# Rows of experts 2 to 7 by way of DRAM and turned on VectorE, and low parts of expert weights formed on VectorE

## The chip, the cores and the metric

The kernel runs on one core of one Trainium2 chip. A core has five engines that run side by side: TensorE (PE in the profile, with its weight loads as PEld), VectorE (DVE), ScalarE (ACT), GpSimd (POOL) and SyncE (SP); here SP only issues DMAs, and POOL issues the indirect ones. The metric is the device time of one execution in microseconds, lower is better. The time before is the median of three runs.

## The reference, cut to what matters

Attention over 8 batches of 2496 tokens with 256 features, then a mixture of 8 experts over all 19968 tokens. All data are float32.

```python
# attention, per batch
scores = (1.0 / S) * np.matmul(z, z.transpose(0, 2, 1))
x = u * np.matmul(np.maximum(scores, 0.0) ** 2, v)
# mixture of experts, x as 19968 x 256
do_compute = x @ w_skip > 0
xc = x[do_compute]
logits = xc @ w_gate
e_idx = np.argmax(logits, axis=1)          # one expert per token
gate_w = softmax(logits)[e_idx]
for e in range(8):
    mask = e_idx == e
    h = np.maximum(xc[mask] @ w1[e], 0.0)  # 256 -> 1024
    y[mask] = gate_w[mask, None] * (h @ w2[e])
out = x.copy()
out[do_compute] = xc + y
```

With the inputs of the run, 10022 tokens go to an expert: 1191, 1245, 1235, 1194, 1290, 1073, 1292 and 1502 to the experts 0 to 7.

## The kernel before

**Precision.** Every large product is made of three PE products of a faster float type: an operand is split into a high part (a cast, on ACT) and a low part (operand minus high part, a subtraction), and high x high, high x low and low x high are summed in PSUM. So weights, activations and rows each need a cast and a subtraction.

**The two stages.** The attention stage fills the first 1260 us. It writes the rows of x to `xr` in DRAM and for each token an entry (token number, gate weight) into the list of its expert, `lst`. The expert stage follows; the change is there.

**Units.** The expert stage works through the experts in order. An expert has three fixed units of 256 tokens each (`NFIX`, two tiles of 128 rows, called a pair here), and then a switch (`tc.Switch`, one arm for each number of 64-token pieces) whose arm holds the units for the rest. In an arm, a unit covers up to 512 tokens: with these counts the arms of experts 2 to 7 hold 8, 7, 4 + 5, 5, 4 + 5 and 8 + 4 pieces, thus 5 or 6 pairs for each expert. `unit` (L609) emits four `h_part`s for a fixed unit (two blocks of 128 of the 1024 hidden features each; PE writes `psh`, ACT the high part `hh`, DVE the low part `hl`), then `y_part`s (PE, `y`), and last `o = y * gate + x` on DVE and the indirect DMA of `o` to the output on POOL. In the first unit of an arm all four first `h_part`s come ahead of the first `y_part`. `psh` has four buffers.

**What else is emitted in a unit.** `fills` maps a slot (0 to 3 after the four `h_part`s, 4 to 6 after the pieces of y, 7 behind them but ahead of `o`) to jobs. Since the order is written by hand, the slot sets the place on every engine that the job uses. The jobs:

- `rows(e, i)`: `fetch` (L580) copies 256 token numbers to `go` on DVE, and POOL gathers the rows from `xr` into the tile `pair(e, i)`, 128 rows per indirect DMA. Four `go` buffers are there.
- `turn_pe` (L596): PE transposes the pair by four transposes of 128x128 into `pst`, ACT casts it to the high part, DVE subtracts for the low part. The result `xt` (`xtf` for an expert's first pair) has the features on the partitions, as PE needs it. Pair i + 1 is turned in slot 3 of unit i, the pairs 3 and 4 both in unit 2, and pair 0 of the next expert in slot 7 of unit 2.
- `wq`, from `load_w` (L126): eight pieces of the next expert's weights, each a DMA of 256 KB by SP into `raw` (four buffers), a cast on ACT and a subtraction (`w1l`, or the second half of `w2t`). The subtraction is on DVE for expert 1's weights, and on POOL for those of experts 2 to 7, which are formed while the expert ahead of them runs.
- `load_ids`: a list from DRAM, on SP.

In one expert, rows of its own pairs 3 to 5 are gathered in slot 1 of its units 0 to 2, and those of the next expert's pairs 0 to 2 in slot 4.

Of the kernel before, what the change touches and what calls it, by code (L numbers as in the profile page):

```python
# [8 lines left out]
F32 = mybir.dt.float32  # L9
# [35 lines left out]
def f32(ap):  # L45
    return ap.bitcast(F32)
# [3 lines left out]
def attn_moe(ctx, tc, zT, uT, v, wg, w1, w2, cst, pad, out):  # L50
# [21 lines left out]
    dram = ctx.enter_context(tc.tile_pool(name="dram", bufs=1, space=bass.MemoryType.DRAM))  # L72
# [102 lines left out]
    nc.gpsimd.memset(ones, 1.0)  # L175
    psw = ps_s.tile([P, 2, QC], F32, name="psw", tag="s")
    for _ in range(NWARM):
        nc.tensor.matmul(psw[:32, 0, :70], ones[:, :32], ones[:, :70], start=True, stop=True)
# [417 lines left out]
    def turn_pe(xg, xt, n=2, o=0, rows64=False):  # L596
# [9 lines left out]
        nc.scalar.copy(xh, ps[:, :, : n * P])  # L606
        nc.vector.tensor_sub(xl, ps[:, :, : n * P], f32(xh))
# [319 lines left out]
    def add(fills, *slots):  # L927
        for k, f in slots:
            fills.setdefault(k, []).append(f)

    def rows(e, i):
        return lambda: fetch(ids_of(e, i), pair(e, i))

    for e in range(E):
        more = e + 1 < E
        wq = load_w(e + 1, nc.gpsimd if e else nc.vector) if more else []
        narms = NARM + (2 if e == 0 else 1)
        for i in range(NFIX):
            fills = {}
            if e:  # L940

                add(fills, (1, rows(e, i + 3)), (3, lambda: turn_pe(pair(e, i + 1), turned(e, i + 1))))
                if e == 1 and i == 0:
                    add(fills, (0, rows(1, 2)))
                if more:
                    add(fills, (4, rows(e + 1, i)))
                if i == 0 and e + 2 < E:
                    add(fills, (6, lambda: load_ids(idts[e + 2], e + 2, 2 * NSTAT)))
                add(fills, *zip((1, 3, 5), wq[3 * i : 3 * i + 3]))
            elif i == 0:  # L950
                add(fills, (0, lambda: turn_pe(pair(0, 1), turned(0, 1))))
                add(fills, (1, gates), (1, logits), (1, route), (2, counts), (2, gate), (2, rows0), (2, rows1),
                    (2, store), (4, store), (5, end_routes), (6, end_lists))
                add(fills, *zip((0, 2), left))
            elif i == 1:
                add(fills, (1, end_counts), (3, lambda: turn_pe(pair(0, 2), turned(0, 2))), (4, rows(0, 3)), (6, rows(0, 4)))
                add(fills, *zip((1, 3, 5), wq[:3]))
            else:
                add(fills, (1, rows(1, 0)), (3, rows(0, 5)), (4, lambda: turn_pe(pair(0, 3), turned(0, 3))),
                    (5, rows(1, 1)), (6, lambda: load_ids(idts[2], 2, 2 * NSTAT)))  # L960
                add(fills, *zip((1, 2, 3, 5, 6), wq[3:]))
            if e and more and i == 2:
                add(fills, (7, lambda: turn_pe(pair(e + 1, 0), turned(e + 1, 0))))
            if i == NFIX - 1:

                add(fills, (5, lambda: turn_pe(pair(e, NFIX + 1), turned(e, NFIX), 2, 2 * P)))
                n = nc.values_load(fin["arm"][0:1, e : e + 1], min_val=0, max_val=narms - 1)  # L967
                add(fills, (1, lambda: tc.switch_hint({g: n for g in ENGINES}, narms, label="rest%d" % e)))  # L968
            ids = ids_of(e, i) if e else idt_e[:, 2 * i : 2 * i + 2, :]
            xg = pair(e, i)  # L970
            unit(e, 4, ids, [xg[:, 0, :], xg[:, 1, :]], turned(e, i), fills)


        for arm in tc.Switch(n, narms, hint="rest%d" % e):  # L974
            ws = widths(arm) if arm <= NARM else []
            if arm > NARM:
                for i in range(NFIX):
                    xg = fetch(ids_of(0, i), xgs["u"][i])
                    turn_pe(xg, xts[0])
                    unit(0, 4, ids_of(0, i), [xg[:, 0, :], xg[:, 1, :]], xts[0])  # L980
            end = NFIX + -(-sum(ws) // 4)
            i, there = NFIX, NFIX + 2
            if e == 0 and not ws:
                turn_pe(pair(1, 0), turned(1, 0))
            for j, hw in enumerate(ws):
                fills = {}
                after = ws[j + 1 :]
                nxt = i + -(-hw // 4)
                if e == 0 and j == 0:
                    add(fills, (1, lambda: turn_pe(pair(1, 0), turned(1, 0))))  # L990
                while there < min(i + 3, end - 1):
                    there += 1
                    add(fills, (1, rows(e, there)))
                if after:
                    xt = xts[(NFIX + j + 1) % 2]
                    add(fills, (3, lambda nxt=nxt, xt=xt: turn_pe(pair(e, nxt), xt)))
                    if after[0] > 4:
                        add(fills, (5, lambda nxt=nxt, xt=xt: turn_pe(pair(e, nxt + 1), xt, 2, 2 * P)))
                w = -(-hw // 2)
                xg = [pair(e, i + t // 2)[:, t % 2, :] for t in range(w)]  # L1000
                unit(e, hw, ids_of(e, i, w), xg, xts[(NFIX + j) % 2], fills, not more and not after, 3 if j else 4)
                i = nxt
            if arm >= NARM:
                ce = nc.values_load(fin["cnt"][0:1, e : e + 1], min_val=0, max_val=N)
                with tc.For_i((NSTAT if arm == NARM else NFIX) * UT, ce, UT) as tok:
                    it = op.tile([P, 2, 2], I32, name="it", tag="it")
                    nc.sync.dma_start(
                        it, lst[bass.ds(tok + e * CAP, UT), :].rearrange("(k p) c -> p k c", p=P)
                    )
                    xg = fetch(it, xgs["u"][0])  # L1010
# [57 lines left out]
```

## Time and profile before

| | |
|---|---|
| median of 3 runs | 1759.48 us (1757.15 to 1759.67) |
| the profiled execution | 1750.08 us, of which the span is 1748.3 us |
| granted TensorE clock | 0.998 |
| busy in 0 to 1262 us | PE 1254.30, DVE 992.69, ACT 979.67, POOL 268.64 us; DMA share 0.73 |
| busy in 1262 to 1748.3 us | PE 475.62, DVE 195.14, ACT 151.87, POOL 251.17 us; DMA share 0.29 |
| DMA | 294.71 MB |

The two stretches are the attention and the expert stage. How its rows are read: a group is line, engine, operation, out<-in and count, then busy time and mean ns of one, then the idle time of the engine just ahead of them and what ended it. A row of the timeline is start and duration in us, engine, line and operation, with the idle time ahead of it in brackets. In a list of waits stand total, number and longest, in us. "DMA issues" give count, KB each and the median us from issue to landing. A line "... x4" joins four instructions.

### The profile page before, as it was taken

The page shows a single profiled execution, that of the slowest core. Times are in us where ns is not written, and L with a number is a line of the kernel's source. Part 1 is how long each engine was busy: PE and PEld are TensorE (multiplying, and loading weights), DVE is VectorE, ACT ScalarE, POOL GpSimd, SP SyncE. Part 2 cuts the span into 40 slices and gives each one's busy share as a digit, 9 for nine tenths or more (in the row PEclk, how much of TensorE's full clock was granted, in tenths as well). Part 3 has the DMA queues.
Part 4 walks back from the last instruction along what each step waited for, and adds up shares of the span by engine and source line. Part 5 has one row for each costly group of instructions (what it writes and reads, how often), then busy time and mean ns, then how long its engine had stood idle before and what let it go on. Part 6 is the DMA issues. An engine that isn't in the chain of part 4 may idle for free. (4 is left out here: it accounts for less than half of the span.)

```text
span 1748.3 us, 39163 instructions
## 1 busy us (share of the span) xinstructions
PE 1729.9 (99%) x15476; PEld 1531.0 (88%) x15476; DVE 1187.8 (68%) x1928; ACT 1131.5 (65%) x1409; POOL 519.8 (30%) x516
## 2 busy tenths in 40 slices
PE   9999999999999999999999999999999999999998
PEld 7888788988888898888889888888999999999997
DVE  7877877887887788788778877877753334344332
ACT  8877877887687778768787876887533323333321
POOL 1103202212311221231222032122256456635731
PEclk9999999999999999999999999999999999999999
DMA  5566779577867858885785888586653333323310
GB/s 194 151 180 173 187 209 275 136 221 233 216 167 202 251 162 231 230 234 148 206 250 163 212 240 228 138 223 190 202 128 81 86 88 106 91 59 97 85 42 26
DMA packets 373514, 294.71 MB, mean 169 GB/s; under 512 B 136432, under 2 KB 311409, under 8 KB 372560
## 3 DMA queue, kind: packets, MB, share of 16 engines
q1 hardware_dynamic: 359136, 267.85, 55.4%
q0 software_dynamic: 13632, 22.99, 4.6%
q8 instruction: 137, 2.24, 0.5%
q14 instruction: 177, 1.45, 0.3%
q10 hardware_dynamic: 432, 0.18, 0.0%
HBM read 177.92 MB, written 133.79 MB: 178 GB/s over the span
## 5 line engine op out<-in xcount | busy, mean ns | idle before, releaser
L366 PE MATMUL acc<-ah,vh 64*128 64x512 f32 (+1 forms) x3120 | 641.5, 384 | 2.7 <-DVE ah L335 2.0
L366 PE MATMUL acc<-ah,vl 64*128 64x512 f32 (+1 forms) x3120 | 626.4, 382 | 0.0
L339 DVE TENSOR_TENSOR al<-r,ah 128x1024 fp32r<-128x1024 f32 (+1 forms) x400 | 479.2, 1204 | 169.6 <-ACT ah L335 163.1
L366 PE MATMUL acc<-al,vh 64*128 64x512 f32 (+1 forms) x3120 | 498.2, 384 | 1.9 <-DVE al L339 1.2
L537 POOL DMA_INDIRECT lst<-pair,dest x160 | 200.0, 1250 | 769.1 <-DVE dest L535 685.1
L335 ACT CAST ah<-r 128x1024 fp32r<-128x1024 f32 (+1 forms) x356 | 362.8, 1030 | 80.9 <-PE acc L366 43.4
L366 PEld LDWEIGHTS acc<-ah,vh 64*128 64x128 f32 x3120 | 326.8, 184 | 56.0 <-ACT ah L335 4.3
L366 PEld LDWEIGHTS acc<-ah,vl 64*128 64x128 f32 x3120 | 327.1, 184 | 44.5 <-DVE vl L122 0.3
L366 PEld LDWEIGHTS acc<-al,vh 64*128 64x128 f32 x3120 | 309.5, 184 | 56.3 <-DVE al L339 11.7
L325 ACT ACTIVATE r<-ps 128x1024 f32<-128x1024 f32 (+1 forms) x248 | 252.7, 1019 | 147.2 <-PE ps L277 129.1
L643 ACT ACTIVATE hh<-psh 128x512 fp32r<-128x512 f32 (+2 forms) x172 | 97.0, 571 | 282.6 <-PE psh L638 261.2
L326 ACT ACTIVATE r<-r 128x1024 f32<-128x1024 f32 (+1 forms) x248 | 261.4, 1054 | 7.9
L657 PE MATMUL y<-w2t,hh 128*128 128x256 f32 (+1 forms) x1328 | 235.0, 280 | 0.0
L644 DVE SCALAR_TENSOR_TENSOR hl<-psh,hh 128x512 fp32r<-128x512 f32 (+2 forms) x172 | 110.2, 655 | 146.7 <-ACT hh L643 130.2
L294 DVE STREAM_TRANSPOSE rt<-r 128x512 f32<-128x512 f32 x304 | 197.3, 687 | 9.4 <-DMA kept<-rt 8.5
L657 PEld LDWEIGHTS y<-w2t,hh 128*128 128x128 f32 (+1 forms) x1328 | 200.5, 185 | 1.3
L638 PE MATMUL psh<-xt,w1h 128*128 128x256 f32 (+3 forms) x896 | 184.6, 303 | 2.9 <-DVE hl L644 2.9
L657 PE MATMUL y<-w2t,hl 128*128 128x256 f32 (+1 forms) x664 | 184.2, 277 | 0.0
L638 PEld LDWEIGHTS psh<-xt,w1h 128*128 128x128 f32 x896 | 141.7, 189 | 8.5 <-DVE hl L644 4.4
L638 PE MATMUL psh<-xt,w1l 128*128 128x256 f32 (+3 forms) x448 | 135.0, 301 | 0.0
L689 POOL DMA_INDIRECT out<-o,idt x77 | 76.5, 994 | 164.2 <-DVE o L686 131.9
L657 PEld LDWEIGHTS y<-w2t,hl 128*128 128x128 f32 (+1 forms) x664 | 122.6, 185 | 0.0
(188 smaller groups left out, 1706.7 us busy)
## 6 DMA issues: line engine op xcount, KB each, us to landing
kept<-rt SPq DMA_DIRECT2D x304, 256.0 KB, 4.8
r<-kept SPq DMA_DIRECT2D x90, 512.0 KB, 6.5
r<-kept SPq DMA_DIRECT2D x62, 352.0 KB, 5.6
raw<-in_v SPq DMA_DIRECT2D x80, 256.0 KB, 5.5
ut<-in_uT SPq DMA_DIRECT2D x32, 512.0 KB, 5.8
xr<-xrow SPq DMA_DIRECT2D x128, 128.0 KB, 3.1
out<-xr SPq DMA_DIRECT2D x32, 512.0 KB, 6.8
raw<-in_w SPq DMA_DIRECT2D x64, 256.0 KB, 3.3
```

Source lines behind the costliest of these rows:

```text
L294: nc.vector.transpose(t[:, :, 32 * k : 32 * k + 32].rearrange("p (k a) i -> p a k i", k=4), r[:, x, :].rearrange("p (a k i) -> p a k i", a ...
L325: nc.scalar.activation(r[:, :, :n], ps[:, :, :n], AF.Relu, scale=isc)
L326: nc.scalar.activation(r[:, :, :n], r[:, :, :n], AF.Square)
L335: (nc.scalar.copy if on_act(ci, p) else nc.vector.tensor_copy)(h_, r_)
L339: nc.vector.tensor_sub(l_, r_, f32(h_))
L366: nc.tensor.matmul(acc[t][:, :n], w[h, x, dd], a[h, x, :n], start=(first and t not in halves[:m]), stop=(last and t not in halves[m + 1 :]),)
L537: put = nc.gpsimd.indirect_dma_start(out=lst, out_offset=bass.IndirectOffsetOnAxis(ap=dest[:, t : t + 1], axis=0), in_=pair[:, t, :], in_o ...
L638: nc.tensor.matmul(ps[:, j * W : (j + 1) * W], wt[:, a, o : o + P], x[:, d, :W], start=(m == 0), stop=(m == 5),)
L643: nc.scalar.activation(hh[:, : G * W], ps[:, : G * W], AF.Relu)
L644: nc.vector.scalar_tensor_tensor(hl[:, : G * W], ps[:, : G * W], 0.0, f32(hh[:, : G * W]), op0=ALU.max, op1=ALU.subtract)
L657: nc.tensor.matmul(ys[t], h[:, tt], w2t[f][:, k, :], start=(f == 0 and m == 0 and t % share == 0), stop=(f == NF - 1 and m == 2), skip_gro ...
L689: put = nc.gpsimd.indirect_dma_start(out=out, out_offset=bass.IndirectOffsetOnAxis(ap=ids[:m, t, 0:1], axis=0), in_=ot, in_offset=None, bo ...
```

## The change

From expert 2 on (`FAR = 2`) a pair of rows goes through DRAM once more. `to_far` writes the gathered pair to a buffer `far` of its expert in DRAM, and `blocks` reads it back by four DMAs into a tile of 32-row blocks, so that one 32x32 block transpose on DVE (`turn_dve`) gives the turned pair, which ACT casts and DVE subtracts as before. PE has no part in it. The features come out in another order, and the rows of `w1` of these experts are put in the same order on the host. All six pairs of an expert are gathered while the expert ahead of it runs, two pairs per unit in slots 1 and 2, in tiles that alternate between two sets. All weights' low parts are formed on DVE. The PE warm-up at the kernel's start has 48 products of 77 columns instead of 52 of 70.

```diff
-NWARM = 52
+NWARM = 48
+FAR = 2
+    far = [[dram.tile([UT, D], F32, name="far%d%d" % (k, i)) for i in range(NSTAT)] for k in range(2)]
...
+    blk, more_rows = [], []
+    def blk_of(i):
+        return blk[i % 2][:, : UT // 32] if i else xgs["u"][2].rearrange("p t (m f) -> p (t m) f", f=64)
+    def blocks(e, i):
+        src = far[e % 2][i].rearrange("(m i) (b f) -> b i m f", i=32, b=4)
+        for b in range(4):
+            nc.sync.dma_start(blk_of(i)[32 * b : 32 * b + 32], src[b])
+    def to_far(e, i):
+        return lambda: nc.sync.dma_start(far[e % 2][i].rearrange("(t p) d -> p t d", p=P), pair(e, i))
+    def turn_dve(e, i, xt, o=0):
+        raw = zp.tile([P, 2 * D], F32, name="xraw", tag="zf", bufs=3)
+        nc.vector.transpose(
+            raw.rearrange("p (d m i) -> p m d i", d=2, i=32),
+            blk_of(i).rearrange("p m (d j) -> p m d j", d=2),
+        )
+        xh, xl = (x[:, :, o : o + UT] for x in xt)
+        r = raw.rearrange("p (d q) -> p d q", d=2)
+        nc.scalar.copy(xh, r)
+        nc.vector.tensor_sub(xl, r, f32(xh))
...
+    def turn(e, i, xt, o=0):
+        return (lambda: turn_dve(e, i, xt, o)) if e >= FAR else (lambda: turn_pe(pair(e, i), xt, 2, o))
+    def to_blocks(e, i):
+        return lambda: blocks(e, i)
     for e in range(E):
         more = e + 1 < E
-        wq = load_w(e + 1, nc.gpsimd if e else nc.vector) if more else []
+        wq = load_w(e + 1, nc.vector) if more else []
         for i in range(NFIX):
             if e:
-                add(fills, (1, rows(e, i + 3)), (3, lambda: turn_pe(pair(e, i + 1), turned(e, i + 1))))
+                if e < FAR:
+                    add(fills, (1, rows(e, i + 3)))
+                else:
+                    add(fills, (0, to_blocks(e, i + 1)))
+                add(fills, (3, turn(e, i + 1, turned(e, i + 1))))
                 if more:
-                    add(fills, (4, rows(e + 1, i)))
+                    add(fills, (1, rows(e + 1, 2 * i)), (2, rows(e + 1, 2 * i + 1)))
+                    if i:
+                        add(fills, (3, to_far(e + 1, 2 * i - 2)), (4, to_far(e + 1, 2 * i - 1)))
+                if e >= FAR and i == 0:
+                    add(fills, (3, to_far(e, 4)), (4, to_far(e, 5)))
+                if e >= FAR and i == NFIX - 1:
+                    add(fills, (0, to_blocks(e, NFIX + 1)), (6, to_blocks(e, NFIX + 2)))
+                if more and i == NFIX - 1:
+                    add(fills, (4, to_blocks(e + 1, 0)), (7, turn(e + 1, 0, turned(e + 1, 0))))
...
-                add(fills, (5, lambda: turn_pe(pair(e, NFIX + 1), turned(e, NFIX), 2, 2 * P)))
+                add(fills, (5, turn(e, NFIX + 1, turned(e, NFIX), 2 * P)))
...
+    w1 = np.concatenate([moe_w1[:FAR], moe_w1[FAR:, cols]])
```

In the arms `turn` stands in the place of `turn_pe` in the same way.

DVE in unit 2 of expert 3, from the third hl to o, in the program before (`xt1` is the pairs 3 and 4 turned for the arm, `xtf` the first pair of expert 4):

```order
L644 SCALAR_TENSOR_TENSOR hl_40854<-psh_40852,hh_40853 128x512
L644 SCALAR_TENSOR_TENSOR hl_40871<-psh_40869,hh_40870 128x512
L607 TENSOR_TENSOR xt1_17733<-pst_40886,xt1_17733 128x2x256
L584 COPY go_40911<-idt4_204 128x2
L607 TENSOR_TENSOR xt1_17733<-pst_40931,xt1_17733 128x2x256
L607 TENSOR_TENSOR xtf_18114<-pst_40962,xtf_18113 128x512
L686 SCALAR_TENSOR_TENSOR o_40969<-y_40763,idt3_203,xgf_18108 128x256 x2
```

And the same place in the changed program:

```order
L673 SCALAR_TENSOR_TENSOR hl_40911<-psh_40909,hh_40910 128x512
L586 COPY go_40926<-idt4_216 128x2
L673 SCALAR_TENSOR_TENSOR hl_40936<-psh_40934,hh_40935 128x512
L629 STREAM_TRANSPOSE xraw_40951<-blk_18126 128x8x2x32
L636 TENSOR_TENSOR xt1_17745<-xraw_40951,xt1_17745 128x2x256
L161 TENSOR_TENSOR w2t_40956<-raw_40757,w2t_40956 128x256
L161 TENSOR_TENSOR w2t_40959<-raw_40757,w2t_40959 128x256
L629 STREAM_TRANSPOSE xraw_40991<-blk_18125 128x8x2x32
L636 TENSOR_TENSOR xt1_17745<-xraw_40991,xt1_17745 128x2x256
L629 STREAM_TRANSPOSE xraw_41023<-xgu_18123 128x8x2x32
L636 TENSOR_TENSOR xtf_18131<-xraw_41023,xtf_18130 128x512
L715 SCALAR_TENSOR_TENSOR o_41027<-y_40812,idt3_215,xgf_18120 128x256 x2
```

Between the last hl and o stood three subtractions and a copy; now there are three transposes, three subtractions of turned rows and two of weights.

SP in expert 3, from its last weights to the switch, in the program before (`raw` is a piece of expert 4's weights):

```order
L578 DMA idt5_205<-lst_88 128x16x2
L97 DMA raw_40621<-in_w2 128x512
L97 DMA raw_40668<-in_w2 128x512
L97 DMA raw_40708<-in_w2 128x512
L967 TENSOR_LOAD arm_18374
L967 ISA x2
L968 SWITCH_STRIDE
L968 ISA
```

And in the changed program, from the last piece of weights on (`far00` to `far03` are pairs 0 to 3 of the successor expert, `far13` to `far15` pairs 3 to 5 of the running one, `xgu_18123` and `blk` the block tiles):

```order
L99 DMA raw_40757<-in_w2 128x512
L1019 TENSOR_LOAD arm_18391
L1019 ISA x2
L621 DMA blk_18126<-far13_100 32x8x64 x4
L621 DMA blk_18125<-far14_101 32x8x64 x4
L1020 SWITCH_STRIDE
L1020 ISA
L1020 BRANCH_PREFETCH_HINT
L624 DMA far02_91<-xgf_17743 128x2x256
L624 DMA far03_92<-xgx_18127 128x2x256
L621 DMA xgu_18123<-far00_89 32x8x64 x4
L621 DMA blk_18126<-far15_102 32x8x64 x4
```

Where SP had nothing left to issue, it now issues two far writes and 16 block reads; the blocks of the successor's first pair stand behind both far writes.

More of the change, by code (lines that the diff above doesn't have):

```diff
@@ L177, in attn_moe @@
     for _ in range(NWARM):
-        nc.tensor.matmul(psw[:32, 0, :70], ones[:, :32], ones[:, :70], start=True, stop=True)
+        nc.tensor.matmul(psw[:32, 0, :77], ones[:, :32], ones[:, :77], start=True, stop=True)
     f0 = load_z(0, 0, nc.vector)
@@ L870, in attn_moe @@
     row_tiles("u", 4)
+    blk += [xp.tile([P, QC // 32, D // 4], F32, name="blk", tag="xrow") for _ in range(2)]
+    more_rows += [xp.tile([P, 2, QC], F32, name="xgx", tag="ut", bufs=3)[:, 0].rearrange("p (t f) -> p t f", t=2) for _ in range(3)]
     xtf += [zp.tile([P, 2, 2 * P], F32R, name="xtf", tag="zl", bufs=ZBUFS) for _ in range(2)]
@@ L950, in attn_moe @@
             elif i == 0:
-                add(fills, (0, lambda: turn_pe(pair(0, 1), turned(0, 1))))
+                add(fills, (0, turn(0, 1, turned(0, 1))))
                 add(fills, (1, gates), (1, logits), (1, route), (2, counts), (2, gate), (2, rows0), (2, rows1),
@@ L955, in attn_moe @@
             elif i == 1:
-                add(fills, (1, end_counts), (3, lambda: turn_pe(pair(0, 2), turned(0, 2))), (4, rows(0, 3)), (6, rows(0, 4)))
+                add(fills, (1, end_counts), (3, turn(0, 2, turned(0, 2))), (4, rows(0, 3)), (6, rows(0, 4)))
                 add(fills, *zip((1, 3, 5), wq[:3]))
             else:
-                add(fills, (1, rows(1, 0)), (3, rows(0, 5)), (4, lambda: turn_pe(pair(0, 3), turned(0, 3))),
+                add(fills, (1, rows(1, 0)), (3, rows(0, 5)), (4, turn(0, 3, turned(0, 3))),
                     (5, rows(1, 1)), (6, lambda: load_ids(idts[2], 2, 2 * NSTAT)))
                 add(fills, *zip((1, 2, 3, 5, 6), wq[3:]))
-            if e and more and i == 2:
-                add(fills, (7, lambda: turn_pe(pair(e + 1, 0), turned(e + 1, 0))))
             if i == NFIX - 1:
-                add(fills, (5, lambda: turn_pe(pair(e, NFIX + 1), turned(e, NFIX), 2, 2 * P)))
+                add(fills, (5, turn(e, NFIX + 1, turned(e, NFIX), 2 * P)))
                 n = nc.values_load(fin["arm"][0:1, e : e + 1], min_val=0, max_val=narms - 1)
@@ L983, in attn_moe @@
             if e == 0 and not ws:
-                turn_pe(pair(1, 0), turned(1, 0))
+                turn(1, 0, turned(1, 0))()
             for j, hw in enumerate(ws):
@@ L989, in attn_moe @@
                 if e == 0 and j == 0:
-                    add(fills, (1, lambda: turn_pe(pair(1, 0), turned(1, 0))))
+                    add(fills, (1, turn(1, 0, turned(1, 0))))
                 while there < min(i + 3, end - 1):
                     there += 1
-                    add(fills, (1, rows(e, there)))
+                    add(fills, (1, rows(e, there)), *([(3, to_far(e, there))] if e >= FAR else []))
                 if after:
                     xt = xts[(NFIX + j + 1) % 2]
-                    add(fills, (3, lambda nxt=nxt, xt=xt: turn_pe(pair(e, nxt), xt)))
-                    if after[0] > 4:
-                        add(fills, (5, lambda nxt=nxt, xt=xt: turn_pe(pair(e, nxt + 1), xt, 2, 2 * P)))
+                    for k in range(2 if after[0] > 4 else 1):
+                        if e >= FAR and nxt + k > NFIX + 2:
+                            add(fills, (2 + 2 * k, to_blocks(e, nxt + k)))
+                        add(fills, (3 + 2 * k, turn(e, nxt + k, xt, 2 * P * k)))
                 w = -(-hw // 2)
@@ L1009, in attn_moe @@
                     )
-                    xg = fetch(it, xgs["u"][0])
-                    turn_pe(xg, xts[0])
+                    xg = xs = fetch(it, xgs["u"][2 if e >= FAR else 0])
+                    if e >= FAR:
+                        xs = zp.tile([P, 2, D], F32, name="xs", tag="zf", bufs=3)
+                        for t in range(2):
+                            nc.vector.tensor_copy(
+                                xs[:, t].rearrange("p (d b j) -> p b d j", d=2, b=4),
+                                xg[:, t].rearrange("p (b d j) -> p b d j", b=4, d=2),
+                            )
+                    turn_pe(xs, xts[0])
                     unit(e, 4, it, [xg[:, 0, :], xg[:, 1, :]], xts[0])
@@ L1052 @@
     pad = pad.reshape(P, 512)
-    ins = dict(zT=zt, uT=uu, v=vv, wg=wg, w1=moe_w1, w2=w2, cst=cst, pad=pad)
+    ins = dict(zT=zt, uT=uu, v=vv, wg=wg, w1=w1, w2=w2, cst=cst, pad=pad)
     nc = bacc.Bacc("TRN2", target_bir_lowering=False, num_devices=1)
```

7 lines of the change are left out of this document (6 added, 1 removed).

## The prediction

> **What bounds the kernel now.** I read the page's busy times first, then the same times for one stretch of the expert stage, then the list of who PE waited for there, then the chain that ended last. Experts are numbered 0 to 7; the change begins at expert 2.
>
> ```profile
> PE 1729.9 (99%) x15476; PEld 1531.0 (88%) x15476; DVE 1187.8 (68%) x1928; ACT 1131.5 (65%) x1409; POOL 519.8 (30%) x516
> ```
> ```profile
> 1377.00:1413.00 36.00, 36.00 (x314) 36.00 (x313) 13.88 (x28) 13.79 (x28) 24.69 (x25) 1.00 0.36 97
> ```
> ```profile
> PE psh L638 <- DVE hl L644: 2.9, 4, 1.5
> PE psh L638 <- DVE o L686: 0.8, 1, 0.8
> ```
>
> The second row is the stretch of the three fixed units of expert 2: 36.00 us, PE busy for all of it at clock 1.00, then PEld, DVE 13.88, ACT 13.79, POOL 24.69, DMA share 0.36. PE is the bound, and in the whole stage it waited 3.7 us: four times for a low part hl from DVE, once for the sum o. So PE work that is taken out shortens the kernel, unless another engine then makes PE wait.
>
> **PE work taken out.**
>
> ```profile
> 1609.20 5.76 PE psh L638 x48
> 1614.96 0.44 PE pst L604 x4
> 1615.39 5.66 PE y L657 x48
> ```
>
> These are rows of the chain that ended last, one unit of 256 rows: four parts of psh, a turn, y. One turn, four transposes, holds PE for 0.44 us. The four have nothing beside them on PE. The profile's groups hold 176 such transposes into pst, 44 turns:
>
> ```profile
> L604 PE MATMUL pst<-ident,xgf 128*128 128x128 f32 x92 | 13.8, 272 | 0.0
> L604 PE MATMUL pst<-ident,xgu 128*128 128x128 f32 x84 | 12.8, 273 | 0.0
> ```
>
> Nine of the 44 belong to experts 0 and 1 and stay on PE. The turn of expert 2's first pair, at 1354.40, is the first of the 35 that move to DVE. **Gain: 35 x 0.44 = 15.4 us.**
>
> **Work put on DVE.** Two groups leave POOL (65.1 us together), and run on DVE at the durations which expert 1's weights already show there:
>
> ```profile
> L159 POOL TENSOR_TENSOR w2t<-raw,w2t 128x256 fp32r<-128x256 f32 x48 | 34.1, 740 | 0.3
> L153 POOL TENSOR_TENSOR w1l<-raw,w1h 128x512 fp32r<-128x512 f32 x24 | 31.0, 1303 | 0.5
> ```
> ```profile
> L159 DVE TENSOR_TENSOR w2t<-raw,w2t 128x256 fp32r<-128x256 f32 x10 | 3.8, 417 | 0.0
> L153 DVE TENSOR_TENSOR w1l<-raw,w1h 128x512 fp32r<-128x512 f32 x4 | 2.7, 687 | 0.0
> ```
>
> 48 x 0.417 + 24 x 0.687 = 36.5 us over six experts, 6.1 each. A turn on DVE is a transpose of 128x512, a copy on ACT and the subtraction that DVE had before. No row shows the new block transpose; the nearest is the one of the attention part with the same size, and I take its 0.69. The ends are 0.65 (197.3 us over 304) and twice 0.69; the upper end adds 0.7 us per turn to the chain below.
>
> ```profile
> L294 DVE STREAM_TRANSPOSE rt<-r 128x512 f32<-128x512 f32 x304 | 197.3, 687 | 9.4 <-DMA kept<-rt 8.5
> ```
> ```profile
> L606 ACT CAST xt<-pst 128x512 fp32r<-128x512 f32 x37 | 21.6, 584 | 20.7 <-PE pst L604 20.7
> L607 DVE TENSOR_TENSOR xt<-pst,xt 128x512 fp32r<-128x512 f32 x37 | 25.3, 683 | 21.3 <-ACT xt L606 21.3
> ```
>
> A turn thus holds DVE for 0.69 + 0.58 (waiting for ACT) + 0.68, about 1.95 us. In the 36 us of the windows row DVE goes from 13.9 to 13.9 + 6.1 + 5 x 0.69 = 23.5 us, with 3 us more of waiting for ACT: it fits as a sum. In the first two units of an expert it also fits in order: after the last hl of a unit come one turn and two pieces of weights, 1.95 + 1.5, and PE has 5.66 us of y before it. Those I cost at nothing; the cover is that y, and each us beyond would be paid once per unit.
>
> **Where DVE comes late: the third unit.** There three turns and a piece follow the last hl, all ahead of o, and DVE goes through the switch to the expert's last units only after o.
>
> ```profile
> 1407.45 0.69 DVE L644 SCALAR_TENSOR_TENSOR hl<-psh,hh 128x512 fp32r<-128x512 f32 x1 [0.72 <-ACT hh L643]
> ```
> ```profile
> 1414.84 0.87 DVE L686 SCALAR_TENSOR_TENSOR o<-y,idt,xgf 128x256 f32<-128x256 f32 x2
> 1418.77 0.69 DVE L644 SCALAR_TENSOR_TENSOR hl<-psh,hh 128x512 fp32r<-128x512 f32 x1 [3.06 <-ACT hh L643]
> ```
> ```profile
> 1412.97 0.60 PE L604 MATMUL pst<-ident,xgf 128*128 128x128 f32 x4
> ```
>
> Expert 2 before: y is done at 1412.97, PE begins the next unit at 1413.41, o ends at 1415.71, 2.3 us after that. Changed, counted from the start of the last hl: y is done at 1412.97 - 1407.45 - 2 x 0.44 = 4.64; DVE does hl (0.6), turn (1.95), piece (0.8), turn (1.95), turn (1.95), o (0.87) and ends at 8.1, 3.4 to 3.5 us after PE began the next unit. So o is 1.1 us later against PE. Then the switch:
>
> ```profile
> 1473.29 0.87 DVE L686 SCALAR_TENSOR_TENSOR o<-y,idt,xgf 128x256 f32<-128x256 f32 x2
> 1476.60 0.62 DVE L644 SCALAR_TENSOR_TENSOR hl<-psh,hh 128x448 fp32r<-128x448 f32 x1 [2.44 <-ACT hh L643]
> ```
> ```profile
> 1473.41 0.55 ACT L643 ACTIVATE hh<-psh 128x448 fp32r<-128x448 f32 x1 [0.76 <-DVE xtf L607]
> ```
>
> In expert 3 ACT's hh was done at 1473.96, yet DVE's first hl began at 1476.60: 2.44 us after o is DVE's own price for the switch, whatever the label says. The first hl of the last units therefore starts 3.4 + 2.44 = 5.84 us after PE began them. PE needs it when its four psh buffers are full:
>
> ```profile
> 1419.51 0.50 PE L638 MATMUL psh<-xt,w1h 128*128 128x512 f32 x1 [0.35 <-DVE hl L644]
> ```
> ```profile
> 1477.27 0.47 PE L638 MATMUL psh<-xt,w1h 128*128 128x448 f32 x1 [0.40 <-DVE hl L644]
> ```
> ```profile
> 1597.20 0.56 PE L638 MATMUL psh<-xt,w1h 128*128 128x320 f32 x2 [1.53 <-DVE hl L644]
> ```
>
> Before, that hl began after 5.36 us in expert 2 (1418.77, held by ACT), and after 2.3 + 2.44 = 4.75 in experts 3 to 6. So PE waits 0.5 us longer in expert 2 and 1.1 each in 3 and 5 (on top of 0.40 and 1.53). In 4 and 6 it did not wait: hl was done after 4.75 + 0.7 = 5.45 us, four parts of psh take 5.76, so 0.3 was to spare and 0.8 each is lost. **Loss: 0.5 + 1.1 + 1.1 + 0.8 + 0.8 = 4.3 us.** Expert 7 turns nothing for a successor and has no weights to form: nothing.
>
> **The way through DRAM.** POOL gathers, SP writes far, SP reads the blocks, in this order on the queues; behind a waiting far stand the blocks of later turns and the weights, and DVE's hl and o wait behind the turn.
>
> ```profile
> 1387.73 1.05 POOL L586 DMA_INDIRECT xgu<-xr,go  x1 [4.82 <-issue]
> 1389.09 1.02 POOL L586 DMA_INDIRECT xgu<-xr,go  x1 [0.30 <-issue]
> ```
> ```profile
> 1327.45 1.05 POOL L586 DMA_INDIRECT xgf<-xr,go  x1 [4.49 <-DVE go L584]
> ```
> ```profile
> 1248.92 2.23 SPq L416 DMA_DIRECT2D xr<-xrow  x4
> ```
> ```profile
> xr<-xrow SPq DMA_DIRECT2D x128, 128.0 KB, 3.1
> ...
> out<-xr SPq DMA_DIRECT2D x8, 448.0 KB, 7.2
> ...
> xgf<-xr,go POOLq DMA_INDIRECT x48, 3.5
> ```
>
> POOL's indirect DMAs follow each other at about 1.33 us, and SP's at 0.56. The tightest turn is that of the next expert's first pair, since its blocks stand behind two far writes of the unit. In expert 2: eight gathers and two outs from 1387.73 end at 1401.0; landing +3.5; five issues +2.2; landing +3.1 (from xr, whose DMAs have the same 256-byte pieces and twice the bytes): 1409.8. DVE comes to that turn at 1407.45 - 0.88 + 5.3 = 1411.9. **Margin 2 us**; the other turns have half a unit or more. In expert 1 POOL has 14 gathers and two outs, because six pairs of expert 2 come on top: 1327.45 + 21.3 = 1348.7, blocks at 1357.5. DVE wants them after the last turn that PE still does there, at 1353. From 1357.5 the turn, o, the switch and hl (1.95 + 0.87 + 2.44 + 0.7) end at 1363.5, and PE wants that hl at 1354.40 + 5.76 = 1360.2:
>
> ```profile
> 1352.39 0.69 DVE L607 TENSOR_TENSOR xt<-pst,xt 128x512 fp32r<-128x512 f32 x1 [2.24 <-ACT xt L606]
> ```
> ```profile
> 1354.40 0.60 PE L604 MATMUL pst<-ident,xgf 128*128 128x128 f32 x4
> ```
>
> PE waits 3.3 us; all its waits before came to 2.9 in four places, 2.3 of them in experts 2, 3 and 5, which leaves 0.6 here: **loss 2.7 us, once.** The 36 far writes and 36 block reads are 18.9 MB; DMA was busy for 0.36, so the idle part covers them. What held SP until now goes with POOL's subtractions:
>
> ```profile
> SPq L97 <- POOL w1l L153: 246.7, 24, 37.8
> ```
>
> SP now waits for DVE's instead, which come within the unit. The warm-up has 3696 columns for 3640, 0.05 us on 3.22, and PE then waited for ACT anyway:
>
> ```profile
> 1.01 3.22 PE L178 MATMUL psw<-ones 128*32 128x70 bf16 x52 [1.01 <-POOL ones L175]
> 4.38 0.50 PE L277 MATMUL ps<-zh 64*128 64x512 f32 x2 [0.16 <-ACT zh L110]
> ```
>
> **A rule weighed.** The Trainium skill, "DMA: Bandwidth & Descriptors", section Specifications, asks for 512 bytes or more per transfer for line rate, and the blocks are read in pieces of 256. If that doubled a block's landing to an estimated 6.2 us, by that page, the margin would be overdrawn by 1.1 us in each of five experts. The xr row above, 3.1 us in such pieces, does not bear it out for writes; no row here shows such reads.
>
> **Sum.** 15.4 - 4.3 - 2.7 = 8.4 us. The profiled execution took 1750.08 us (span 1748.3), so it becomes 1741.7. The median of the runs shown is 1759.48, 9.4 above the profiled one; taking the same 8.4 us off gives **1751.1 us**. I call 0.2% (3.5 us) the least that a measurement of this kernel tells from no change.
>
> **Rivals.**
> - *Nothing is lost on DVE*: its turns overlap ACT better than I let them, or the switch is reached early, since the next expert's turn no longer waits for the end of y. Then all 15.4 us come back: 1744.1. For it: DVE idles half the stretch. Against it: everything after the last hl is in order, and o stands last. 0.14.
> - *The switch costs twice*: the block transpose takes 1.4 us, or ACT, which came through the switch only at 1418.06 in expert 2, holds hh as long in all five. Loss 8.6 instead of 4.3: 1755.4, near the limit of no change. 0.12.
> - *Blocks late, slower*: if the blocks land not 3.1 but 7.2 us after issue, as the slowest group above, the first-pair turn is 2.1 us late in five experts (10.5) and 4.1 more in expert 1: 1751.1 + 14.6 = 1765.7. It becomes slower than before from a landing of about 6 us. For it: five such turns with 2 us to spare. Against: the stage's DMA share of 0.36. 0.10.
> - *The change does less than it says*: PE's end could hang on the last scatters. Against it: PE was busy for all of the windows row. 0.02, no change.
>
> **How the numbers follow.** My forecast, 1747.5 to 1755.5, has 0.62; the others as given, a third of the second rival counted as faster. Faster 0.62 + 0.14 + 0.04 = 0.80, no change 0.08 + 0.02 = 0.10, slower 0.10. The range 1743 to 1758 takes in the first two rivals and leaves out the third.
>
> **What would show it.** Right: 36 PE transposes into pst left (nine turns); DVE block transposes near 0.69 us; PE's waits for hl at five switches of 0.8 to 2.6 us and one near 3.3 in expert 1; block reads landing in about 3 us. Wrong: DVE waiting for block reads in the first units of an expert, PE waiting for xt inside the fixed units, or raw weights late because SP stands behind a far write.

## The result, and the profile after

| | kernel before | changed kernel | ratio, 95% interval |
|---|---|---|---|
| first measurement | 1759.58 (1757.15 to 1759.80, 4 runs) | 1787.98 (1782.47 to 1792.55, 4 runs) | 1.0166 [1.0139, 1.0192] |
| second, on another occasion | 1756.94 (15 runs) | 1787.10 (5 runs) | 1.0182 [1.0160, 1.0204] |
| third, on another again | 1745.22 (23 runs) | 1736.74 (4 runs) | 0.9943 [0.9924, 0.9961] |

The change was forecast to take 8.4 us off and came out 28 us slower. The third row is the same kernel, and there it is 8.5 us faster. The occasions on which kernels ran are of two kinds, and the time of the kernel before tells them apart: about 1757 to 1759, or about 1745. One chip was of the one kind at one time and of the other later, so the kind does not belong to the chip. Below, an occasion of the first kind is called **stalling** and one of the second **quiet**, for what their traces show: on a stalling one PE stands still again and again without a semaphore to hold it. Ratios are always against the kernel before on the same occasion.

The first three lines are from the page of the changed kernel in the first measurement (stalling; its execution took 1792.55, span 1790.8), the fourth from the page on the quiet occasion (1738.2, span 1736.3), where the PE and PEclk rows are nines up to the last slice of PE:

```profile
PE 1741.5 (97%) x15332; PEld 1539.6 (86%) x15332; DVE 1235.3 (69%) x2035; ACT 1133.5 (63%) x1409; POOL 454.6 (25%) x444
...
PE   9999999999999999999999999999897999999998
...
PEclk9999999999999999999999999999998999999999
```
```profile
PE 1716.1 (99%) x15332; PEld 1526.5 (88%) x15332; DVE 1236.0 (71%) x2035; ACT 1134.1 (65%) x1409; POOL 456.0 (26%) x444
```

The same 15332 matmuls: 1716.1 us of PE time when quiet, 13.8 below the 1729.9 of before, and 1741.5 when stalling. The spans differ by 54.5 us; 25.4 of them are in PE's busy time, the other 29.1 PE is idle. The stretches of the stage (whole core; PE, PEld, DVE, ACT, POOL, then clock and DMA share) put it all behind 1262:

```profile
0.00:1262.00 1262.00, 1256.24 (x11659) 1075.31 (x11660) 995.39 (x1545) 980.60 (x1109) 270.31 (x264) 1.00 0.73 203
1262.00:1791.00 529.00, 485.23 (x3676) 464.24 (x3674) 239.91 (x490) 152.91 (x300) 184.29 (x181) 0.96 0.41 109
```
```profile
0.00:1262.00 1262.00, 1256.97 (x11678) 1079.37 (x11679) 997.25 (x1556) 982.13 (x1113) 271.82 (x266) 1.00 0.73 203
1262.00:1737.00 475.00, 459.10 (x3656) 447.13 (x3654) 238.71 (x480) 151.96 (x297) 184.18 (x179) 0.99 0.46 122
```

Who PE waited for from 1240 on, stalling and then quiet (total us, times, longest):

```profile
PE y L686 <- issue: 15.8, 27, 1.7
PE psh L667 <- issue: 5.6, 7, 1.9
PE psh L667 <- DVE hl L673: 4.0, 2, 2.3
PE y L686 <- ACT hh L672: 3.9, 4, 1.2
```
```profile
PE psh L667 <- DVE hl L673: 6.5, 4, 4.1
PE psh L667 <- DVE o L715: 0.8, 1, 0.8
PE psh L667 <- DVE xt L636: 0.7, 3, 0.3
```

"Issue" means that no semaphore the profile shows held PE back. The shown rows make it 21.4 us of the stalling trace; the quiet one has none. With one of 0.4 us that is not shown there are 35 such waits, and 28 of them stand before instructions that wait for no semaphore at all. What it looks like, in expert 1 (PE, and POOL from the first to the last issue of its run; in brackets the idle time before):

```profile
1343.54 0.39 PE L686 MATMUL y<-w2t,hh 128*128 128x256 f32 x2
1343.76 0.28 PE L686 MATMUL y<-w2t,hl 128*128 128x256 f32 x1
1343.88 0.61 PE L686 MATMUL y<-w2t,hh 128*128 128x256 f32 x2
1345.53 0.28 PE L686 MATMUL y<-w2t,hl 128*128 128x256 f32 x1 [1.05 <-issue]
1345.65 0.28 PE L686 MATMUL y<-w2t,hh 128*128 128x256 f32 x1
1346.95 0.38 PE L686 MATMUL y<-w2t,hh 128*128 128x256 f32 x1 [1.01 <-issue]
...
1352.64 0.37 PE L686 MATMUL y<-w2t,hh 128*128 128x256 f32 x1 [1.72 <-issue]
1353.37 0.58 PE L686 MATMUL y<-w2t,hl 128*128 128x256 f32 x1 [0.35 <-issue]
1354.77 0.56 PE L686 MATMUL y<-w2t,hh 128*128 128x256 f32 x1 [0.83 <-issue]
1356.17 0.37 PE L686 MATMUL y<-w2t,hh 128*128 128x256 f32 x1 [0.83 <-issue]
1356.86 0.37 PE L686 MATMUL y<-w2t,hl 128*128 128x256 f32 x1 [0.32 <-issue]
```
```profile
1333.84 1.46 POOL L588 DMA_INDIRECT xgf<-xr,go  x1 [4.64 <-DVE xt L609]
1335.60 1.01 POOL L588 DMA_INDIRECT xgf<-xr,go  x1 [0.30 <-issue]
...
1353.96 1.00 POOL L588 DMA_INDIRECT xgx<-xr,go  x1 [0.30 <-issue]
```

Until 1343.9 PE starts a matmul every 0.12 us. From then on it stands still, and its starts after most pauses lie close to whole multiples of 0.71 us apart: 1345.53, 1346.95, 1348.39, 1349.83, and at the end 1352.64, 1353.37, 1354.77, 1356.17, 1356.86. That began 10 us after POOL had started a run of 16 indirect DMAs without a break, and ended 2 us after the run's last one. SP's register instructions at the switch, which the page doesn't count, start 0.59 to 0.71 us apart from 1349.90 on, four of the five steps 0.70 or 0.71; the same ones in expert 2 start 0.06 to 0.09 apart. ACT's hh of the stretch comes late as well.

Then the clock. The granted clock was halved for 13.65 us here, and five more times for 3.4 to 6.8 us before the end, 41 us in all; the first two:

```profile
1347.50:1361.15 13.65, 8.55 (x32) 6.93 (x31) 3.39 (x8) 2.89 (x7) 5.93 (x6) 0.50 0.57 172
1422.60:1429.40 6.80, 5.59 (x25) 5.53 (x26) 3.65 (x9) 1.84 (x5) 1.17 (x2) 0.50 0.91 234
```

It follows the stalls and is not their start: at 1343.88 to 1347.5 PE stalls at the full clock. The Trainium skill, "TensorE: Matmul & The Clock Gate", Part 1, says that the gate knows only full and half rate and decides by windows of 3413 ns; the trace agrees: but for the last stretch, which the end of the program cuts off, all halved stretches are multiples of 3.4 us.

### The profile page after: what moved, and what is told of

It reads as the page before. It is cut to its first block, busy times and chain, and to the rows that moved or that the text cites. A ratio compares the mean times of both kernels' runs of the same rounds, so it can differ in the third digit from the quotient of the medians.

```text
span 1790.8 us, 39261 instructions
## 1 busy us (share of the span) xinstructions
PE 1741.5 (97%) x15332; PEld 1539.6 (86%) x15332; DVE 1235.3 (69%) x2035; ACT 1133.5 (63%) x1409; POOL 454.6 (25%) x444
## 2 busy tenths in 40 slices
DMA packets 422478, 313.62 MB, mean 175 GB/s; under 512 B 176176, under 2 KB 360369, under 8 KB 421520
## 4 chain that ended last, share of the span: by engine, by line
PE 79%; DMA 7%; issue 5%; ACT 4%; DVE 3%; another core or an unknown queue 1%; POOL 1%; POOLq 0%; SPq 0%; DVEq 0%; ACTq 0%
PE acc L368 53%; PE ps L279 9%; PE psh L667 8%; PE y L686 7%; DMA out<-o,idt 3%; DMA xgu<-xr,go 2%; DVE al L341 1%; PE psm L440 1%; ACT ah L337 1%; DMA r<-kept 1%; ACT r L328 1%; ACT r L327 1%; ACT hh L672 0%; DVE rt L296 0%
## 5 line engine op out<-in xcount | busy, mean ns | idle before, releaser
L368 PEld LDWEIGHTS acc<-ah,vh 64*128 64x128 f32 x3120 | 331.4, 184 | 51.9 <-ACT ah L337 3.9
L368 PEld LDWEIGHTS acc<-ah,vl 64*128 64x128 f32 x3120 | 331.9, 184 | 42.6 <-DVE vl L124 0.3
L368 PEld LDWEIGHTS acc<-al,vh 64*128 64x128 f32 x3120 | 314.8, 184 | 52.9 <-DVE al L341 10.0
L686 PE MATMUL y<-w2t,hh 128*128 128x256 f32 (+1 forms) x1328 | 248.1, 287 | 14.0 <-issue 9.8
L686 PEld LDWEIGHTS y<-w2t,hh 128*128 128x128 f32 (+1 forms) x1328 | 210.0, 192 | 23.1 <-issue 15.1
L686 PE MATMUL y<-w2t,hl 128*128 128x256 f32 (+1 forms) x664 | 191.1, 288 | 8.9 <-issue 6.1
L686 PEld LDWEIGHTS y<-w2t,hl 128*128 128x128 f32 (+1 forms) x664 | 127.1, 191 | 10.6 <-issue 6.7
```

Source lines behind the costliest of these rows:

```text
L368: nc.tensor.matmul(acc[t][:, :n], w[h, x, dd], a[h, x, :n], start=(first and t not in halves[:m]), stop=(last and t not in halves[m + 1 :]),)
L686: nc.tensor.matmul(ys[t], h[:, tt], w2t[f][:, k, :], start=(f == 0 and m == 0 and t % share == 0), stop=(f == NF - 1 and m == 2), skip_gro ...
```

## The experiments

**First group (quiet, kernel before 1745.84).** Three theories were set against each other: that long runs of POOL's issues stall the others (A), that the traffic through DRAM does (B, later T1), that VectorE is late (C).

```diff
 low_on_pool
-        wq = load_w(e + 1, nc.vector) if more else []
+        wq = load_w(e + 1, nc.gpsimd if e else nc.vector) if more else []
 spread_gathers
-    add(fills, (1, rows(e + 1, 2 * i)), (2, rows(e + 1, 2 * i + 1)))
+    add(fills, (1, rows(e + 1, 2 * i)), (5, rows(e + 1, 2 * i + 1)))
 before_low_dve (to the kernel before)
-        wq = load_w(e + 1, nc.gpsimd if e else nc.vector) if more else []
+        wq = load_w(e + 1, nc.vector) if more else []
 no_far_pe_turn
-        return (lambda: turn_dve(e, i, xt, o)) if e >= FAR else (lambda: turn_pe(...))
+        return lambda: turn_pe(pair(e, i), xt, 2, o)
     to_far and to_blocks return lambda: None; w1 = moe_w1
```

> The change as it is, with the low parts of the weights of experts 2 to 7 back on POOL (the DVE turn and the way through DRAM stay). Theory A (bunched gathers): PE, ACT and SP stall while POOL issues indirect DMAs without a break; the changed kernel has such runs of 10, 16, 10, 10 and 10 issues beside its five longest stalls, because two pairs are gathered per unit and no low part stands between them any more. With the low parts back between the gathers the runs fall to 4 or less, most of the 41 us at half clock goes, and the time is 1745 to 1762. Theory B (the DMA traffic through DRAM, 18.9 MB more in pieces of 256 bytes and 1 KB): nothing in the DMA queues changes, so 1780 to 1792 with some 40 us at half clock. Theory C (VectorE, given 36 us of low parts, is late with hl): 36 us of work leave VectorE, the waits for hl and xt go, about 4 us, and the time is 1778 to 1785.

> The change as it is, with the second of the two gathers that each fixed unit issues for the next expert moved from fill place 2 to fill place 5 of its unit. Theory A: the longest run of POOL's indirect DMAs falls from 16 to about 6, the stalls shrink to a third, and the time is 1755 to 1772. Theory B: the same bytes in the same units, so 1778 to 1792. Theory C: VectorE's work is untouched, 1783 to 1792.

> The kernel before, with the low parts of the weights of experts 2 to 7 on VectorE alone (rows fetched and turned as before). Theory A: the runs of indirect DMAs stay at 4, as in the kernel before, so no stalls and 1755 to 1764. Theory B: no DMA is added, 1755 to 1764 as well. Theory C: VectorE takes 36 us more and is late with hl and o at the switches, 1765 to 1785.

> The change with its gathers a whole expert ahead and its low parts on VectorE, but without the writes to DRAM and the block reads: all experts' rows are turned by PE's transposes out of the gathered rows, 35 turns by 0.44 us = 15.4 us more on PE than in the changed kernel. Theory A: the runs of gathers are the same, so the stalls stay (about 40 us) and the time is 1785 to 1805. Theory B: the added traffic is gone, so is the stall, and the time is 1755 to 1766. Theory C: as the changed kernel with 15 us more on PE, 1790 to 1805.

Measured: 1770.46, 1.0146 [1.0125, 1.0168]; 1740.94, 0.9970 [0.9960, 0.9980]; 1742.84, 0.9980 [0.9971, 0.9990]; 1742.42, 0.9982 [0.9973, 0.9992]. Read as they were meant, they spoke against all three theories: the kernel with the longest runs of issues (no_far_pe_turn, 26) showed no stall, and the one without them was slow. Two edits did not shorten or leave the runs as expected: spread_gathers still had one of 24 issues, before_low_dve one of 16. The loss of low_on_pool was another one (the waits of DVE, then PE, then SP from 1315 on):

```profile
DVE xraw L629 <- DMA xgu<-far: 19.7, 6, 5.9
```
```profile
PE psh L667 <- DVE hl L673: 17.5, 4, 6.4
PE y L686 <- DVE hl L673: 5.3, 2, 3.5
```
```profile
SPq L99 <- POOL w1l L155: 192.9, 16, 35.2
SPq L624 <- DMA xgx<-xr,go: 6.7, 2, 3.9
```

With 65 us of low parts in POOL's queue again the blocks of the next expert's first pair are late: DVE waits up to 5.9 us for them and PE up to 6.4 for the hl behind. In expert 1 it is a gather, for which SP waits 3.9 us before a far write. From expert 2 on it is SP's own queue: a weight's DMA (L99) waits until POOL has subtracted the piece ahead in its buffer, and the far writes and block reads stand behind it. In expert 2 SP so waited until 1405.55, issued the blocks of two other pairs, and came to the far writes at 1411.0, where it waited for nothing. That is the outcome of the rival of the late blocks, by late issue and not by slow landing. What the group lacked was the changed kernel itself, and hence what kind of occasion it was.

**Second group (stalling, 1756.94).**

> The changed kernel itself once more, unaltered, beside its own profile: is what it lost a property of the kernel? Theory T1 (the added DMA traffic, together with gathers of two pairs close after another, stalls PE, ACT and SP): the ratio to the kernel before is 1.012 to 1.020, as in the first measurement, with some 40 us at half clock in the middle units. Theory T2 (the stalls come with the chip or the execution and not with the kernel): the ratio is 0.995 to 1.003 and there is less than 8 us at half clock before the last instruction.

> The kernel before, unaltered, profiled on the same chip as the runs beside it. Both theories: a ratio of 0.998 to 1.002. T1: no stalls of PE in steps of 0.7 us after 1250. T2: if the chip brings them, the kernel before shows some too, and its time on such a chip is 10 us or more above 1746.

> All the DMA traffic of the change (the writes to DRAM and the block reads, at their places), its gathers and its low parts on VectorE, but the blocks are read into their tiles and used by nothing: experts 2 to 7 are turned by PE's transposes out of the gathered rows. Beside it stands the kernel without that traffic (1742.4 beside 1745.8 for the kernel before). T1: the traffic brings the stalls back, ratio 1.010 to 1.030. T2: the traffic costs nothing, ratio 0.996 to 1.002. A third theory, T3 (what stalls is the turn that waits for the blocks, on VectorE and behind it hl and PE): no turn waits for blocks here, so 0.996 to 1.002 too, while the changed kernel itself stays at 1.012 to 1.020.

```diff
 unread_blocks
-        return (lambda: turn_dve(e, i, xt, o)) if e >= FAR else (lambda: turn_pe(...))
+        return lambda: turn_pe(pair(e, i), xt, 2, o)
     w1 = moe_w1; to_far and to_blocks stay
```

Measured: 1.0182 [1.0160, 1.0204]; 1.0011 [1.0000, 1.0021]; 1784.15, 1.0157 [1.0142, 1.0173]. T3 fell: no turn waits for a block in unread_blocks, and it is as slow. The kernel before is not free of stalls on such an occasion; the largest entry of PE's waits from 1240 on, a run of POOL, and PE in the first expert unit, at the end of the attention:

```profile
PE psh L638 <- issue: 6.2, 9, 1.9
```
```profile
1249.72 1.00 POOL L586 DMA_INDIRECT xgf<-xr,go  x1 [7.32 <-DMA xr<-xrow]
...
1258.84 0.97 POOL L537 DMA_INDIRECT lst<-pair,dest  x1 [0.30 <-issue]
```
```profile
1257.02 0.50 PE L638 MATMUL psh<-xt,w1h 128*128 128x256 f32 x2 [0.97 <-issue]
...
1258.48 0.38 PE L638 MATMUL psh<-xt,w1l 128*128 128x256 f32 x1 [0.27 <-issue]
...
1259.20 0.37 PE L638 MATMUL psh<-xt,w1h 128*128 128x256 f32 x1 [0.21 <-issue]
1259.93 0.57 PE L638 MATMUL psh<-xt,w1l 128*128 128x256 f32 x1 [0.36 <-issue]
```

Eight issues without a break, no far write anywhere, and 7 us into them the same grid (1257.02, 1258.48, 1259.20, 1259.93). So the stall does not need the change; on such an occasion the changed kernel has more long runs, and more stalls.

**Third group (quiet, 1745.22)**, which repeated three kernels beside the changed one:

> The changed kernel unaltered, as the yardstick of this group. So far the chips have been of two kinds: on one the kernel before took 1757 and showed steps of 0.7 us in PE, on the other it took 1746 and showed none. Theory A (PE, ACT and SP stall some 8 us after POOL began to issue indirect DMAs without a break, on chips of the first kind): 1.012 to 1.020 on a chip of the first kind, and 0.996 to 1.002 on one of the second. Theory T1 (the traffic through DRAM does it): 1.012 to 1.020 on either.

Measured: the changed kernel 0.9943 [0.9924, 0.9961]; with spread gathers 0.9974 [0.9961, 0.9988]; without the way through DRAM 0.9975 [0.9966, 0.9985]; the kernel before with low parts on VectorE 0.9985 [0.9976, 0.9995]. This is the whole change and its parts without stalls: the low parts' move gives 0.15%, the way through DRAM and the DVE turns another 0.3% over the kernel without them. POOL's longest run in the changed kernel was then 24 issues, and PE waited on issue for nothing:

```profile
1322.28 1.04 POOL L588 DMA_INDIRECT xgf<-xr,go  x1 [4.44 <-DVE hl L673]
...
1353.05 1.00 POOL L588 DMA_INDIRECT xgx<-xr,go  x1 [0.30 <-issue]
```

**Fourth group (quiet, 1745.15)**, meant for a stalling one. Without DRAM and with spread gathers it gave 0.9982 each, as before. The third:

```diff
 pauses_on_pool
     def go():
         fetch(ids_of(e, i), pair(e, i))
+        for _ in range(16 if e >= FAR else 0):
+            nc.gpsimd.memset(pz, 0.0)
```

> The changed kernel with sixteen small memsets on POOL (a tile that nothing reads) behind each pair's two gathers for the experts 2 to 7, so that POOL issues at most two gathers, and the scatters of a unit, in a row. The traffic is the same; gathers and scatters go out some 2 to 4 us later. Theory A: on a chip that stalls the runs above 4 are gone from expert 1 on, the half-clock time before the last instruction falls below 12 us, and the ratio is 0.995 to 1.008. Theory T1: the same bytes, 1.012 to 1.022. On a chip that does not stall 0.994 to 0.999 by both.

Measured 1794.26, 1.0286 [1.0267, 1.0305], outside of what either theory gave: each set of sixteen memsets held POOL for 3.6 us, and the blocks came later still (DVE, then PE, from 1315 on). Here it was the gathers: SP's far writes waited for them 18 times, 88.5 us in all. On this occasion it says nothing on the stalls; it prices the margin of the way through DRAM.

```profile
DVE xraw L629 <- DMA xgu<-far: 46.1, 6, 10.6
```
```profile
PE psh L667 <- DVE hl L673: 34.5, 4, 10.5
```

**Fifth group (stalling, 1759.45).**

> The change without its way through DRAM, all turns on PE, gathers bunched as in the change, once more, for a chip that stalls (the kernel before at about 1757). Theory A (POOL's unbroken runs of indirect DMAs do it): 1.008 to 1.025 there. Theory T1 (the traffic through DRAM is needed): 0.995 to 1.002 there. On a chip that does not stall (the kernel before at about 1745): 0.998.

> The change with the second gather of each fixed unit at fill place 5 in place of 2, for a chip that stalls. Theory A: stalls begin some 8 us into a run and a run of 8 issues lasts 10.3 us, so a part of them stays, 1.000 to 1.010. Theory T1: the same bytes as the changed kernel, 1.012 to 1.020. On a chip that does not stall: 0.997 to 0.999.

Measured: 1782.77, 1.0141 [1.0111, 1.0171]; 1797.06, 1.0211 [1.0174, 1.0248]. PE's waits without the way through DRAM, from 1315 on:

```profile
PE y L686 <- issue: 14.7, 19, 1.2
PE psh L667 <- issue: 2.2, 2, 1.3
PE pst L606 <- issue: 1.7, 3, 0.8
```

T1 falls: no byte of the added traffic, 18.6 us of waits on issue, and a ratio that can't be told from the 1.0157 with all of the traffic. Spreading missed its forecast on A's side too, and lies above T1's: its runs are of 6 to 10 issues, shorter but more of them. It waited 22.1 us on issue from 1315 on where the changed kernel of the first measurement had 18.1, and it had eleven halved stretches before the end in place of six. So the longest run alone does not set the loss; the changed kernel was not run beside it on this occasion.

**Sixth group (stalling, 1757.48; the chip of the first group, later).**

> The kernel before with the low parts of experts 2 to 7 on VectorE alone. Its longest runs of indirect DMAs from expert 1 on are 14 to 16, 10, 6 to 8, 6 to 8, 6 and 10 issues; a run of n issues takes 1.32 n us, and so far stalls came to about the part of a run behind its first 8 us: 10 to 13, 5, 0 to 3, 0 to 3, 0 and 5 us. Theory A on a chip that stalls (the kernel before at about 1757): 1.006 to 1.015. Theory D (on such a chip it is the gathers a whole expert ahead, not the run's length): 0.997 to 1.002. On a chip that does not stall (1745) both give 0.998.

> The change with the low parts of experts 2 to 7 back on POOL, between the gathers: runs of 4 to 6 issues. On a chip that does not stall it was 1.0146, with PE waiting up to 6.4 us for hl at the switches since blocks landed late. Theory A on a chip that stalls: the same late blocks and few stalls in steps of 0.7 us, 1.012 to 1.020, waits of PE on issue below 6 us from 1340 on where the changed kernel has 20. Theory D: late blocks and the stalls of the changed kernel together, 1.030 to 1.040.

Measured: 1765.71, 1.0054 [1.0034, 1.0074]; 1781.26, 1.0140 [1.0122, 1.0158]. The first is slower, against D, by a little less than A's figures, which took its runs from a quiet trace; here they were one of 10, three of 8, the rest 6 and less. The second, PE from 1315 on:

```profile
PE psh L667 <- DVE hl L673: 18.9, 4, 5.3
PE y L686 <- DVE hl L673: 7.8, 3, 3.7
PE y L686 <- ACT hh L672: 3.1, 2, 2.3
PE psh L667 <- issue: 2.2, 6, 0.8
```

Low parts between the gathers: 2.2 us on issue where the changed kernel had about 18 from 1315 on, and the late blocks in their place. The ratio is that of the quiet occasion (1.0146): without long runs from expert 1 on, a stalling occasion takes no more from this kernel than from the kernel before. D falls.

**All traces together.** The ratios of each kernel on both kinds of occasion, with the longest runs of POOL's issues from expert 1 on in the stalling trace:

| | longest runs | quiet | stalling |
|---|---|---|---|
| changed kernel | 16, 10 | 0.9943 | 1.0166, 1.0182 |
| with spread gathers | 10, 8 | 0.9970, 0.9974, 0.9982 | 1.0211 |
| with the way through DRAM, but turned on PE (unread_blocks) | 16, 10 | not run | 1.0157 |
| without the way through DRAM | 16, 8 | 0.9982, 0.9975, 0.9982 | 1.0141 |
| kernel before, low parts on VectorE | 10, 8 | 0.9980, 0.9985 | 1.0054 |
| changed kernel, low parts on POOL | 6 | 1.0146 | 1.0140 |

For every run of POOL's indirect DMAs behind 1240 (less than 0.5 us idle between two issues) all steps of 0.4 to 2.2 us from one PE start to the next are summed, from the run's start to 2.5 us past its end. A length goes from the first start to the last end:

| issues in the run | length, us | 8 stalling traces: runs, mean pause | 12 quiet traces: runs, mean pause |
|---|---|---|---|
| 4 | 5.1 | 76, 0.2 us | 89, 0.1 us |
| 6 | 7.7 | 41, 0.8 us | 11, 0.4 us |
| 8 | 10.5 | 25, 2.9 us | 14, 0.0 us |
| 10 | 13.2 | 9, 4.9 us | 20, 0.0 us |
| 16 | 21.3 | 4, 11.8 us | 13, 0.3 us |

The two columns part at 8 issues. In the stalling traces the pause is about the part of the run beyond its first 8 to 9 us, and the first pause comes 6 to 11 us into the run; each of the 38 runs of 8, 10 and 16 issues has one. In the quiet ones 47 such runs have hardly any, nor have seven of 24 and 26 issues. VectorE's added work does not do it by itself: in the six stalling traces with all low parts on VectorE, 31 runs of 4 issues behind 1315 have 0.2 us on the mean.

## Why the prediction was wrong, point by point

- *PE is the bound, and 35 turns are 15.4 us*: right. 36 transposes into pst are left, and on the quiet occasion PE's busy time fell by 13.8 us, although a 6.8 us stretch there ran at half clock.
- *Work put on DVE*: right. The block transpose, 0.69 forecast, took 0.70; the copy on ACT 0.62; low parts 0.42 and 0.68 as costed.

```profile
L629 DVE STREAM_TRANSPOSE xraw<-blk 128x512 f32<-128x512 f32 x29 | 20.4, 702 | 0.0
L635 ACT CAST xt<-xraw 128x512 fp32r<-128x512 f32 x29 | 18.0, 621 | 41.3 <-DVE xraw L629 41.3
```

- *Loss at the switches, 4.3 us more*: too high. On the quiet occasion PE waited 0.2 us at expert 2's switch, 0.6 at 3's, 1.8 at 5's and for nothing at 4's and 6's, 0.4 us in all above the 0.35, 0.40 and 1.53 it had waited at these switches before. In expert 3 o ended 3.4 us after PE began the next unit, as forecast, but DVE's first hl began 1.88 us after o and not 2.44.
- *Blocks late in expert 1, 2.7 us, once*: right in place and mechanism, too small. DVE waited 5.03 us for the blocks of expert 2's first pair, PE 4.06 for the hl behind, and a halved clock came on top, which I had not costed. It was halved from 1357.0, within that wait, to 1363.8; PE was busy for 4.7 us of it, so it is worth about 2.4:

```profile
1352.98 0.71 DVE L629 STREAM_TRANSPOSE xraw<-xgu 128x512 f32<-128x512 f32 x1 [5.03 <-DMA xgu<-far]
```
```profile
1359.10 1.22 PE L667 MATMUL psh<-xt,w1h 128*128 128x512 f32 x2 [4.06 <-DVE hl L673]
```

 The quiet sum is 15.4 - 0.4 - 3.5 (4.06 less the 0.6 that it waited here before) - 2.4 = 9.1 us; measured 8.5 by the medians (6.8 to 13.3 by the interval), forecast 8.4. That the forecast fits even there is in part luck: the switches were costed 3.9 us too high, expert 1 with its clock 3.2 too low.
- *The 18.9 MB cost nothing*: borne out on both kinds of occasion, as far as these runs can tell. Blocks in 256-byte pieces were no bound either: on the quiet occasion they landed 3.4 us (blk) and 3.6 us (xgu) after issue by the median, near the 3.1 assumed and far from the 6.2 of the rule weighed. What made blocks late in pauses_on_pool was POOL's queue ahead of them, and in low_on_pool mostly SP's, held up by POOL's low parts.
- *POOL*: **the step that failed.** The 65.1 us that leave POOL were counted as pure relief and the gathers, at 1.33 us each, only as a matter of when rows land. I wrote down "eight gathers and two outs" and "14 gathers and two outs" in a row, and asked how late the last one is, not what a queue without a break does to other engines. The sum put that at nothing. On the stalling occasion of the first measurement PE waited 21.4 us on issue and ran 41 us at half clock, where the kernel before, on a stalling occasion, had 6.6 and 6.8 from 1240 on. Nothing in the profile I argued from showed that such a queue does anything: that execution was a quiet one.
- *The anchor*: the forecast of 1751.1 took the 8.4 us off a median that lies 9.4 above the profiled execution, without asking what the 9.4 us are. The two kinds of occasion are the likely answer: on a stalling one the kernel before itself waits on issue, 6.6 us of PE time in its profile. By these marks profile and median were of two different kinds, and a cost that the change makes larger was in the difference.
- *Rivals*: the slower one (late blocks at every first-pair turn, 1765.7) names a real weakness, 1.0146 when POOL is kept busy otherwise, but it is not what happened. The rival in which nothing is lost on DVE (0.14) was nearly right about the switches, 0.4 us, and wrong about expert 1.

**Left open.** What makes an occasion stalling was not found: the kernels, the instruction counts (39261 for the changed one) and the bytes moved (313.62 MB) are the same. One difference goes through all 20 traces. In the eight stalling ones records of semaphore updates are missing: 22025 in place of 25893 for the kernel before, 24036 and 23973 in place of 28747 for the changed one, and of those due before 1240 us about 8% are missing already. So the stalls may have to do with the recording itself, but that is not shown: every time on record comes with a span and a clock of the profiler. Nor is it shown what PE, ACT and SP share with POOL's issues; the grid of 0.71 us is the only trace of it. The kernel with pauses, which shortens the runs and leaves VectorE's work as it is, never ran on a stalling occasion. And the best version depends on the occasion: the changed kernel on a quiet one, the kernel before on a stalling one; no kernel here beats both on both.

## What to carry to other kernels

Look at how many indirect DMAs stand in POOL's queue without other work between them before moving that work away: here runs of 4 had 0.2 us of pauses or less on every kind of occasion, and on the stalling ones those of 8 to 16 had 3 to 12 us each. Cutting them into more runs of 6 to 10 did not help. When a profiled execution and the median of the runs are further apart than the gain you expect, find out what the difference is before taking the gain off either. A verdict from one occasion can have the wrong sign; repeat both kernels on another before believing a mechanism.

## What the hardware showed that was not expected

- With POOL issuing indirect DMAs back to back, PE's and SP's instructions pause and start on a grid of about 0.71 us after some 6 to 11 us, without any semaphore to explain it, on some occasions (1757 to 1759 for the kernel before) and not on others (1745). All eight traces with such pauses lack records of semaphore updates, and none of the twelve others does.
- The same chip was quiet at one time (1745.84) and stalling at another (1757.48).
- A wait of PE of about 4 us is paid again in part: on the quiet occasion PE waited 4.06 us until 1359.10, the granted clock was halved from 1357.0 to 1363.8, and 4.7 us of PE's work fell into it.
